# A gated linear recurrence with a two-branch maximum layer: the issue order of all queues remade, eleven float32 products on zeros at other places

## The chip, the cores and the metric

The kernel runs on one core of a Trainium2 chip. The core has five engines that run side by side, each with a queue of its own that is worked off in order: TensorE (PE in the profile, with PEld for its weight loads), VectorE (DVE), ScalarE (ACT), GpSimd (POOL) and SyncE (SP), which here only issues transfers. Sixteen DMA engines move data between HBM and the core. The metric is the device time of one execution in microseconds (us).

## The reference

The input has 4 batches, 8 heads, 768 time steps and 48 values per head. For every batch and head a 48 x 48 state is carried over the steps, and the result goes through a layer with two weight matrices, a maximum and an output matrix:

```
f = 1.0 / (1.0 + np.exp(-f_logit))
for t in range(S):
    state = f[:, :, t, :, None] * state + np.einsum('bhd,bhe->bhde', k[:, :, t], v[:, :, t])
    y[:, :, t] = np.einsum('bhd,bhde->bhe', q[:, :, t], state)
x = y.transpose(0, 2, 1, 3).reshape(B * S, H * D)      # 3072 x 384
g = np.maximum(x @ w1, x @ w2)                         # w1, w2: 384 x 1024
out = g @ w_out                                        # w_out: 1024 x 384
```

## The kernel before, in words

**Pieces.** The 768 steps of a batch are cut into three windows of 256, which makes 12 pieces, numbered 0 to 11; piece s belongs to batch s mod 4. A piece is one row of partitions for every two time steps, and its two halves of 128 steps (64 partitions each) are two links of the recurrence. The maximum is computed as `max(a, b) = b + relu(a - b)`: one product with w1 - w2 (called wd), a relu, and two products that end in one sum, with w_out and with w2 @ w_out (called m2). wd and m2 are made on the chip, once, at the start.

**Steps.** Every piece of work is a word of the string ORDER. Its letters name a step, then come the numbers of the piece (and of the part), a letter for the engine where there is a choice (a = ACT, v = DVE, p = POOL, s = SP), and `@` with a PSUM bank or an SBUF slot. A loop at the end of the kernel (`for key, of, e, b in words(ORDER)`) calls the steps in that order. There is no other scheduler: the order of the words of one engine is the order of its queue, and waits between engines follow from the data and from the reuse of banks, slots and buffers.

- Loads, all on SP: `Lf Lk Lq Lv` bring f_logit, k, q or v of one piece (393 KB, L137) into one of 22 slots; `Wa Wb` bring half of w1 or w2 (786 KB, L151), `Wo` half of w_out (L155). A load into a slot waits until the slot's earlier content has been read.
- Gates: `E F G` on ACT (exp, log, exp; L275, L279, L283), `e` adds two rows (L286), `C` is the product that sums the logarithms along time (L290, L293), `X Z` on ACT take the exponentials inv and dec (L300, L305).
- Scaled inputs: `i j` scale the even rows of k and q in place (L309, L313), `K Q` write bf16 copies scaled by inv and dec (L320, L323), `V` writes v as bf16 in three copies (L114).
- Recurrence: `t u` transpose K and Q on PE into two banks (L349), `U` copies both to SBUF (L114), `A` are the products of the two (L376), `m` masks them (L384), `S` multiplies with the state (L406), `y` with the values (L426); `D` makes what is added to the state (L440), `n N` update it (L452, L454, L457). `z` reads one column of each bank that `S` wrote, so that the reading engine is in step.
- Layer: `H Y` bring y into the layout of x (L114, L472), `d` with four parts is x times wd (L484), `r` the relu over two parts (L491, L493), `o` the two products that end in one sum (L499, L502), `b` copies it to SBUF (L114), `O` stores it (L520). The last half piece is stored in two halves of columns: `P B R` (L530, L533, L114, L541). `R` issues one transfer on SP and one on ACT's queue.
- Weights: `ws wp we` make wd (L575, L583, L114), `wc wt wx` transpose w2 (L114, L551), `wo` casts w_out, `wm wn` make m2 (L567, L114).
- `J` with a count: products of a 128 x 128 tile of zeros with four copies of itself in float32 (L595), into a bank that is then overwritten. They compute nothing that is used. A float32 product appears as two matmul instructions in the trace.

Of the kernel before, what the change touches and what calls it, by code (L numbers as in the profile page):

```python
# [17 lines left out]


ORDER = """  # L20
Lf0s@12 Lk0s@13 Lq0s@14 Lv0s@15 J4@7 E0a Wb0s F0a Lf1s@12 G0a i0v Wb1s e0v C0@0 J2@7 Wa0s X0a Wa1s
Z0a K0v V0p j0v t0@0 J1@7 Lq1s@13 D0@2 Q0v Lv1s@15 n0.0v u0@0 J2@7 E1a n0.1v U0v@0 F1a e1p A0.0@0
wc1a A0.1@2 m0.0v@0 S0@4 G1a Lk1s@12 wc0a C1@6 z0v@4 wt1@7 ws1v wc2a m0.1v@2 wp1@0 wx1a@7 ws3v y0
Z1a Wo0s ws0v we1a@0 wp3@2 H0a@4 ws2v wt2@7 we3a@2 Wo1s wp0@0 j1v X1a wp2@2 Y0v@4 Q1p we0a@0
Lf2s@0 wt0@6 wx2a@7 we2v@2 d0.0@0 d0.1@1 i1v V1a K1v d0.2@2 Lf4s@13 r0.0a@0 u1@4 wx0v@6 t1@4 wo1p
d0.3@3 U1v@4 wo0p D1@0 r0.1a@2 Lq2s@9 n1.0v A1.0@6 A1.1@4 wo3a wo2v S1@2 n1.1v Lk2s@10 m1.0v@6
wm0@0 E2a z1v@2 m1.1v@4 Lv2s@11 wm2@1 F2a E4a e2p y1 Lk4s@0 F4a C2@4 H1v@2 wm1@5 Y1v@2 Z2a e4p G2a
Lq4s@13 wn0a@0 C4@6 X2a d1.0@2 i2v wn2a@1 j2v wn1a@5 d1.1@3 Lf3s@8 Z4a Q2v d1.2@0 X4a G4a K2v
d1.3@1 V2a Lf5s@9 u2@4 t2@4 r1.1a@0 i4v o0.0@6 U2v@4 K4p Lv4s@11 r1.0a@2 j4v A2.0@0 b0.0a@6
Lq3s@10 D2@2 N1.1p o0.1@4 n2.0v E3a m2.0v@0 Q4p Lv3s@0 F3a n2.1v S2@0 b0.1a@4 A2.1@2 z2v@0 E5a  # L30
t4@6 N0.1p m2.1v@2 Lk3s@13 u4@6 N2.1p o1.0@5 F5a U4v@6 V4a Lf6s@9 e5v G5a y2 j3v b1.0a@5 D4@2
A4.0@6 H2a@0 O0s n4.0v o1.1@5 m4.0v@6 N4.0p Lk5s@11 V3a e3p Lv5s@8 n4.1v G3a Y2v@0 C5@6 b1.1a@5
C3@7 i3p X5a S4@2 Z3a A4.1@4 Lq5s@0 z4v@2 d2.0@0 Z5a Q3v X3a d2.1@1 E6a K3v d2.2@6 r2.0a@0 m4.1v@4
d2.3@7 Lq6s@13 t3@0 r2.1a@6 u3@0 i5p y4 D3@4 U3a@0 Lk6s@9 H4v@2 K5p o2.0@6 n3.0v Y4v@2 Lf8s@10 F6a
n3.1v S3@0 b2.0v@6 A3.0@2 e6p A3.1@4 m3.0v@2 d4.0@6 Lf7s@11 N4.1p d4.1@7 j5v V5p d4.2@2 z3v@0
r4.0a@6 Lk8s@12 m3.1v@4 d4.3@3 G6a D5@6 Q5v r4.1a@2 y3 O1s C6@5 j6v H3a@0 o2.1@4 Lv6s@0 Z6a i6v
E8a Y3v@0 Lq8s@8 X6a F8a t5@2 N3.1v u5@2 b2.1v@4 Lv7s@10 d3.0@0 U5a@2 e8v d3.1@1 n5.0v Q6v d3.2@4
K6v E7a d3.3@5 Lq7s@13 C8@2 N5.0v r3.1a@4 o4.0@3 r3.0v@0 V6p F7a Lf10s@9 n5.1v G8a e7v N5.1p D6@0
Z8a A5.0@4 b4.0v@3 X8a t6@6 Lf9s@0 j8v u6@6 C7@2 U6a@6 n6.0v o3.0@3 m5.0v@4 N6.0p Lk7s@11 V7p
n6.1v X7a i8v A5.1@0 b3.0a@3 A6.0@6 S5@4 Lf11s@10 j7v Z7a K8p o3.1@3 z5v@4 m5.1v@0 Lq9s@15 m6.0v@6  # L40
y5 S6@0 Q8v H5a@4 Lv8s@12 A6.1@6 G7a o4.1@2 E9a z6v@0 i7p m6.1v@6 F9a Y5v@4 b3.1a@3 y6 e9p E10a
O3s t8@6 u8@6 K7p H6a@0 d5.0@3 Lk9s@9 U8v@6 G9a Lq10s@0 b4.1a@2 C9@5 d5.1@4 X9a O4s Y6v@0 Z9a
N6.1p d5.2@6 r5.0a@3 O2s d5.3@7 Q7v d6.0@0 r5.1a@6 Lk11s@11 j9v A8.0@2 Lq11s@13 Q9p D7@4 V8a
m8.0v@2 u7@6 t7@6 d6.1@1 U7a@6 n7.0v Lv9s@12 d6.2@2 N7.0v n7.1v d6.3@3 j10v E11a o5.0@4 r6.0v@0
r6.1a@2 N7.1v A7.0@0 Lv11s@10 b5.0a@4 D8@2 A7.1@6 F11a n8.0v S7@4 m7.0v@0 o6.0@3 F10a e11p
Lk10s@15 G10a z7v@4 N8.0p m7.1v@6 e10p C11@0 Lv10s@8 b6.0a@3 S8@1 i9v A8.1@6 V9p o5.1@3 z8v@1
m8.1v@6 K9v C10@6 y7 Z10a b5.1v@3 D9@7 j11v H7a@4 y8 O5s Z11a Y7v@4 o6.1@3 X11a Q11p H8a@1 n9.0v
Y8v@1 d7.0@4 b6.1a@3 i10p G11a d7.1@5 O6s i11v d8.0@0 r7.0a@4 Q10v d8.1@1 N9.0v X10a d8.2@2 V10a
K10v d8.3@3 r8.0a@0 K11v d7.2@4 d7.3@5 r8.1v@2 u10@6 r7.1a@4 t9@0 u9@0 t10@6 t11@2 U9a@0 U10v@6
u11@2 o8.0@4 U11v@2 A9.0@0 b8.0a@4 S9@2 m9.0v@0 A9.1@6 D10@4 o7.1@5 z9v@2 m9.1v@6 V11v A11.0@0 y9  # L50
n10.0v D11@6 o7.0@4 n11.0v m11.0v@0 N11.0p H9v@2 o8.1@0 b7.0v@4 N10.0v b7.1a@5 Y9v@2 O7s A10.0@6
b8.1a@0 S10@4 m10.0v@6 A10.1@2 d9.0@0 z10v@4 d9.1@1 m10.1v@2 d9.2@6 r9.0a@0 d9.3@7 A11.1@0 r9.1a@6
S11@2 y10 z11v@2 m11.1v@0 o9.0@6 H10a@4 Y10v@4 y11 b9.0a@6 d10.0@0 H11v@2 d10.1@1 d10.2@4 r10.0v@0
o9.1@6 Y11v@2 d10.3@5 d11.0@0 r10.1a@4 d11.1@1 b9.1a@6 d11.2@2 O9s d11.3@3 O8s o10.0@4 r11.1v@2
r11.0v@0 o10.1@3 o11.0@0 b10.0a@4 b10.1a@3 O10s P11.0@1 b11.0a@0 O11s P11.1@0 B11.0v@1 R11.0s
B11.1a@0 R11.1s
"""


# [10 lines left out]
def kernel(  # L70
# [14 lines left out]
    nc = tc.nc  # L85
    B, H, S, D = q.shape
    C = 128
# [17 lines left out]
    banks = psum.tile([C, 8, 512], F32, name="banks")  # L105
# [18 lines left out]
    def load(nm, s, e, slot):  # L124
        w, b = divmod(s, B)
        rows = slice(w * W, (w + 1) * W)
        if s % 2 == 0 and (nm, s + 1) not in alone:

            n = 2
            src = sources[nm][b:b + 2, :, rows, :].rearrange("b h (p two) d -> (b h) p (two d)", two=2)  # L130
            dst = slots[:, slot:slot + 2, :].rearrange("p s (h x) -> p (s h) x", h=H)
            dst = bass.AP(dst.tensor, dst.offset, [list(dst.ap[i]) for i in (1, 0, 2)])
        else:
            n = 1
            src = sources[nm][b, :, rows, :].rearrange("h (p two) d -> p h (two d)", two=2)
            dst = slots[:, slot, :].rearrange("p (h x) -> p h x", h=H)
        engines[e].dma_start(out=dst, in_=src)  # L137
        for i in range(n):
            loaded[s + i][nm] = slots[:, slot + i, :].rearrange("p (h two d) -> p h two d", h=H, two=2)
# [20 lines left out]
    idle = consts.tile([C, C], F32, name="idle")  # L160
# [101 lines left out]
    m2 = consts.tile([C, KT, HD], BF16, name="m2")  # L262
# [327 lines left out]
        ps = banks[:, b:b + 2, :].rearrange("p b x -> p (b x)")[:, 0:KT * n]  # L590
        copy(e, wd[:, :, part * n:(part + 1) * n], ps.rearrange("p (k x) -> p k x", k=KT))

    def step_J(n, b):
        for _ in range(n):
            nc.tensor.matmul(out=banks[:, b, :], lhsT=idle, rhs=idle.unsqueeze(1).to_broadcast([C, 4, C]), start=True, stop=True)  # L595

    steps = {
        "J": lambda n, e, b: step_J(n, b),
        "Lf": lambda s, e, b: load("f", s, e, b), "Lk": lambda s, e, b: load("k", s, e, b),
        "Lq": lambda s, e, b: load("q", s, e, b), "Lv": lambda s, e, b: load("v", s, e, b),  # L600
        "Wa": lambda i, e, b: load_columns(w1_f, moe_w1, e, i),
# [59 lines left out]
```

## Time and profile before

| | |
|---|---|
| median of 3 runs | 140.78 us (140.59 to 141.03) |
| the profiled execution | 140.61 us, of which the span from the first to the last instruction is 138.8 us |
| PE busy in the span | 129.0 us (93%), 2349 matmuls |
| DVE, ACT, POOL busy | 110.1, 87.2, 47.2 us |
| HBM read, written | 23.59 MB, 4.72 MB |
| DMA engines | busy over nine tenths from slice 2 to slice 29 of 40 |

The profile is one execution. A line of a group names the kernel's line, engine, operation, what it writes and reads, the count, then the busy time, the mean of one in ns, and the idle time of the engine just before. Times in timelines count from the start of the span. "Issue" is time in which an engine waited for nothing that the profile shows. A matmul's end is modelled, so its start is the better mark.

### The profile page before, as it was taken

The page shows a single profiled execution, that of the slowest core. Times are in us where ns is not written, and L with a number is a line of the kernel's source. Part 1 is how long each engine was busy: PE and PEld are TensorE (multiplying, and loading weights), DVE is VectorE, ACT ScalarE, POOL GpSimd, SP SyncE. Part 2 cuts the span into 40 slices and gives each one's busy share as a digit, 9 for nine tenths or more (in the row PEclk, how much of TensorE's full clock was granted, in tenths as well). Part 3 has the DMA queues.
Part 4 walks back from the last instruction along what each step waited for, and adds up shares of the span by engine and source line. Part 5 has one row for each costly group of instructions (what it writes and reads, how often), then busy time and mean ns, then how long its engine had stood idle before and what let it go on. Part 6 is the DMA issues. An engine that isn't in the chain of part 4 may idle for free.

```text
span 138.8 us, 5409 instructions
## 1 busy us (share of the span) xinstructions
PE 129.0 (93%) x2349; PEld 92.1 (66%) x2349; DVE 110.1 (79%) x197; ACT 87.2 (63%) x145; POOL 47.2 (34%) x68
## 2 busy tenths in 40 slices
PE   6968779897999999999999999999999999999990
PEld 3335469564866687768666787677886668678570
DVE  5677799996978997999999899799888894861510
ACT  3623899659988989499883999716873115304220
POOL 7434205405096348610583943476200100000000
PEclk9999999999999999999999999999999999999999
DMA  4999999999999999999999999999500021000754
GB/s 104 272 326 341 387 288 285 357 257 250 266 264 253 275 275 252 246 288 260 237 271 217 245 235 313 279 269 228 126 0 5 5 56 58 5 5 20 209 130 97
DMA packets 56248, 28.66 MB, mean 206 GB/s; under 512 B 50464, under 2 KB 54688, under 8 KB 56224
## 3 DMA queue, kind: packets, MB, share of 16 engines
q1 hardware_dynamic: 56064, 28.22, 81.2%
q8 instruction: 18, 0.29, 0.9%
q10 hardware_dynamic: 160, 0.10, 0.3%
q14 instruction: 6, 0.05, 0.1%
HBM read 23.59 MB, written 4.72 MB: 204 GB/s over the span
## 4 chain that ended last, share of the span: by engine, by line
PE 74%; DMA 9%; ACT 4%; issue 4%; DVE 3%; POOL 2%; SPq 1%; ACTq 0%; DVEq 0%; POOLq 0%
PE banks L502 22%; PE banks L484 21%; PE banks L499 9%; DMA slots<-in_moe_w_dram 6%; PE banks L349 4%; PE banks L376 4%; PE banks L426 4%; PE banks L406 3%; DMA slots<-in_f_logit_dram 3%; PE banks L440 2%; PE banks L290 2%; ACT wd L114 1%; POOL wo L114 1%; SPq L151 1%; PE banks L567 1%
## 5 line engine op out<-in xcount | busy, mean ns | idle before, releaser
L502 PE MATMUL banks<-wo,gT 128*128 128x384 bf16 x184 | 33.7, 326 | 0.0
L484 PE MATMUL banks<-xT,wd 128*128 128x256 bf16 x288 | 33.6, 273 | 0.0
L384 DVE TENSOR_TENSOR at_m<-banks,mask 128x1024 bf16<-128x1024 f32 x24 | 29.0, 1216 | 1.5 <-PE banks L376 1.0
L484 PEld LDWEIGHTS <-wd 128*128 128x128 bf16 x288 | 27.3, 98 | 3.8
L502 PEld LDWEIGHTS <-gT 128*128 128x128 bf16 x184 | 18.0, 98 | 11.9
L491 ACT ACTIVATE gT<-banks 128x1024 bf16<-128x1024 f32 x18 | 18.4, 1032 | 11.9 <-PE banks L484 11.5
L114 ACT COPY ob<-banks 128x384 f32<-128x384 f32 (+1 forms) x19 | 8.9, 468 | 19.7 <-PE banks L502 14.5
L499 PE MATMUL banks<-m,xT 128*128 128x384 bf16 x69 | 15.1, 328 | 0.0
L472 DVE SCALAR_TENSOR_TENSOR xT<-tail,gaps,banks 128x256 bf16<-128x256 bf16 x36 | 15.0, 471 | 0.0
L275 ACT ACTIVATE gate<-slots 128x768 f32<-128x768 f32 x12 | 10.2, 847 | 7.0 <-DMA slots<-in_f_logit_dram 7.0
L114 POOL CAST vb<-slots 128x384 bf16<-128x384 f32 (+2 forms) x15 | 8.5, 604 | 12.1 <-DVE state L457 7.0
L457 POOL TENSOR_TENSOR state<-tmp_s,dec 128x256 bf16<-128x256 f32 x10 | 6.8, 680 | 17.2 <-DVE tmp_s L452 17.2
L286 POOL TENSOR_TENSOR e<-ell 128x384 bf16<-128x384 f32 x8 | 8.0, 999 | 13.2 <-ACT ell L279 13.2
L595 PE MATMUL banks<-idle 128*128 128x512 f32 x18 | 10.8, 738 | 1.1 <-DVE idle L161 1.1
L493 DVE TENSOR_SCALAR gT<-banks 128x1024 bf16<-128x1024 f32 x6 | 7.2, 1217 | 4.3 <-PE banks L484 4.3
L323 POOL TENSOR_TENSOR qp<-slots,dec 128x768 bf16<-128x768 f32 x4 | 7.3, 1818 | 9.6 <-DVE slots L313 6.7
L376 PE MATMUL banks<-trs 48*64 48x128 bf16 x384 | 10.1, 220 | 0.3 <-DVE trs L114 0.3
L279 ACT ACTIVATE ell<-gate 128x768 f32<-128x768 f32 x12 | 10.0, 846 | 0.4
L114 ACT COPY trs<-banks 128x2048 bf16<-128x2048 bf16 x5 | 9.3, 1864 | 0.3 <-PE banks L349 0.3
L114 DVE COPY trs<-banks 128x2048 bf16<-128x2048 bf16 x7 | 8.4, 1218 | 1.3 <-PE banks L349 1.3
L376 PEld LDWEIGHTS <-trs 48*64 48x64 bf16 x384 | 7.1, 106 | 3.5 <-issue 2.0
L320 POOL TENSOR_TENSOR kp<-slots,inv 128x768 bf16<-128x768 f32 x4 | 7.5, 1864 | 3.7 <-DVE slots L309 3.5
(76 smaller groups left out, 199.8 us busy)
## 6 DMA issues: line engine op xcount, KB each, us to landing
slots<-in_f_logit_dram SPq DMA_DIRECT2D x12, 384.0 KB, 5.9
slots<-in_k_dram SPq DMA_DIRECT2D x12, 384.0 KB, 5.8
slots<-in_q_dram SPq DMA_DIRECT2D x12, 384.0 KB, 5.9
slots<-in_v_dram SPq DMA_DIRECT2D x12, 384.0 KB, 5.8
out_dram<-ob SPq DMA_DIRECT2D x22, 192.0 KB, 3.1
slots<-in_moe_w_dram SPq DMA_DIRECT2D x4, 768.0 KB, 8.5
slots<-in_moe_w_out_dram SPq DMA_DIRECT2D x2, 768.0 KB, 7.5
out_dram<-ob SPq DMA_DIRECT2D x2, 96.0 KB, 2.2
```

The lines of the kernel that those rows point to most:

```text
L114: (nc.scalar.copy if e == "a" else engines[e].tensor_copy)(out, in_)
L275: nc.scalar.activation(flat(gate[s]), flat(loaded[s]["f"]), AF.Exp, bias=0.0, scale=-1.0)
L279: nc.scalar.activation(flat(ell[s]), flat(gate[s]), AF.Ln, bias=1.0, scale=1.0)
L286: engines[e].tensor_add(pad("e", s)[:, :, 0:D], ell[s][:, :, 0, :], ell[s][:, :, 1, :])
L376: nc.tensor.matmul(out=ps[h * HC:(h + 1) * HC, j % 2, par, :], lhsT=t[rows, 0, h, j, par, :], rhs=t[rows, 1, h, j], start=True, stop=True, ...
L384: nc.vector.tensor_mul(at[s][:, jj].rearrange("p r j a t -> p (r j) (a t)"), banks[:, b:b + 2, :].rearrange("p r (j x) -> p (r j) x", j=2) ...
L472: engines[e].scalar_tensor_tensor(out=x[:, kt], in0=tails[s], scalar=gaps[:, kt:kt + 1], in1=ps[:, :, kt], op0=ALU.mult, op1=ALU.add)
L484: nc.tensor.matmul(out=ps[:, f, :], lhsT=wd[:, kt, ff * C:(ff + 1) * C], rhs=xT[g][:, kt, :], start=(kt == 0), stop=(kt == KT - 1))
L491: nc.scalar.activation(dst, src, AF.Relu)
L499: nc.tensor.matmul(out=ps, lhsT=xT[g][:, kt, cols], rhs=m2[:, kt, :], start=(kt == 0), stop=False)
L502: nc.tensor.matmul(out=ps, lhsT=gT[g][:, ff, cols], rhs=wo[:, ff, :], start=False, stop=(ff == FG - 1))
L595: nc.tensor.matmul(out=banks[:, b, :], lhsT=idle, rhs=idle.unsqueeze(1).to_broadcast([C, 4, C]), start=True, stop=True)
```

## The change

The string ORDER is written anew: nearly every word stands elsewhere. The amount of each kind of step is the same; what differs is the order, many engines, banks and slots, and the zero products. `J` gets a width, and a second step `I` makes the same product with two copies of the tile in place of four, half as wide. Before there were nine zero products, all of `J` (4, 2, 1 and 2); after there are seven of `J` (4, 2 and 1) and four of `I` (1, 1 and 2), eleven in all.

The engines' shares change like this (steps, before and after):

| step | before | after |
|---|---|---|
| K on DVE, POOL | 8, 4 | 5, 7 |
| Q on DVE, POOL | 8, 4 | 6, 6 |
| i on DVE, POOL | 8, 4 | 3, 9 |
| V on ACT, DVE, POOL | 6, 1, 5 | 7, 5, 0 |
| b on ACT, DVE | 18, 5 | 13, 10 |
| r on ACT, DVE | 18, 6 | 21, 3 |
| H on ACT, DVE | 8, 4 | 6, 6 |
| N on DVE, POOL | 6, 10 | 5, 11 |
| wo on ACT, DVE, POOL | 1, 1, 2 | 3, 1, 0 |
| wc on ACT, DVE | 3, 0 | 2, 1 |
| wn on ACT, DVE | 3, 0 | 2, 1 |
| ws on DVE, POOL | 4, 0 | 3, 1 |

The diff, with the opening and the end of the order:

```diff
@@ -18,42 +18,42 @@
 ORDER = """
-Lf0s@12 Lk0s@13 Lq0s@14 Lv0s@15 J4@7 E0a Wb0s F0a Lf1s@12 G0a i0v Wb1s e0v C0@0 J2@7 Wa0s X0a Wa1s
-Z0a K0v V0p j0v t0@0 J1@7 Lq1s@13 D0@2 Q0v Lv1s@15 n0.0v u0@0 J2@7 E1a n0.1v U0v@0 F1a e1p A0.0@0
-wc1a A0.1@2 m0.0v@0 S0@4 G1a Lk1s@12 wc0a C1@6 z0v@4 wt1@7 ws1v wc2a m0.1v@2 wp1@0 wx1a@7 ws3v y0
-Z1a Wo0s ws0v we1a@0 wp3@2 H0a@4 ws2v wt2@7 we3a@2 Wo1s wp0@0 j1v X1a wp2@2 Y0v@4 Q1p we0a@0
-Lf2s@0 wt0@6 wx2a@7 we2v@2 d0.0@0 d0.1@1 i1v V1a K1v d0.2@2 Lf4s@13 r0.0a@0 u1@4 wx0v@6 t1@4 wo1p
-d0.3@3 U1v@4 wo0p D1@0 r0.1a@2 Lq2s@9 n1.0v A1.0@6 A1.1@4 wo3a wo2v S1@2 n1.1v Lk2s@10 m1.0v@6
-wm0@0 E2a z1v@2 m1.1v@4 Lv2s@11 wm2@1 F2a E4a e2p y1 Lk4s@0 F4a C2@4 H1v@2 wm1@5 Y1v@2 Z2a e4p G2a
-Lq4s@13 wn0a@0 C4@6 X2a d1.0@2 i2v wn2a@1 j2v wn1a@5 d1.1@3 Lf3s@8 Z4a Q2v d1.2@0 X4a G4a K2v
-d1.3@1 V2a Lf5s@9 u2@4 t2@4 r1.1a@0 i4v o0.0@6 U2v@4 K4p Lv4s@11 r1.0a@2 j4v A2.0@0 b0.0a@6
...
-b8.1a@0 S10@4 m10.0v@6 A10.1@2 d9.0@0 z10v@4 d9.1@1 m10.1v@2 d9.2@6 r9.0a@0 d9.3@7 A11.1@0 r9.1a@6
-S11@2 y10 z11v@2 m11.1v@0 o9.0@6 H10a@4 Y10v@4 y11 b9.0a@6 d10.0@0 H11v@2 d10.1@1 d10.2@4 r10.0v@0
-o9.1@6 Y11v@2 d10.3@5 d11.0@0 r10.1a@4 d11.1@1 b9.1a@6 d11.2@2 O9s d11.3@3 O8s o10.0@4 r11.1v@2
-r11.0v@0 o10.1@3 o11.0@0 b10.0a@4 b10.1a@3 O10s P11.0@1 b11.0a@0 O11s P11.1@0 B11.0v@1 R11.0s
-B11.1a@0 R11.1s
+J4@7 Lf0s@12 Lk0s@13 Lq0s@14 Lv0s@15 E0a Wb0s F0a Wa0s G0a e0v Lf1s@12 i0v C0@0 J2@7 Z0a j0v X0a
+Wb1s Q0v Wa1s K0v u0@0 I1@7 V0v t0@0 I1@7 Lk1s@13 U0v@0 D0@6 I2@3 n0.0v A0.0@0 A0.1@2 m0.0v@0 S0@4
+J1@0 ws0p z0v@4 Lq1s@15 m0.1v@2 E1a ws1v y0 wp0@0 Lv1s@12 H0a@4 n0.1v F1a Y0v@4 N0.1p wp1@2 we0a@0
+e1p we1v@2 wc1a C1@0 wc0v d0.0@6 wc2a ws2v wt1@1 Wo1s d0.1@7 G1a ws3v Z1a wt0@2 i1p r0.0a@6 wp2@3
+wx1v@1 Wo0s X1a wt2@5 we2a@3 j1v wp3@6 Lf2s@0 Q1v wx0a@2 d0.2@0 K1v u1@3 we3a@6 V1v wx2a@5 t1@3
+d0.3@1 U1v@3 Lf4s@13 D1@6 wo2a n1.0v A1.0@2 S1@4 m1.0v@2 wo3a r0.1a@0 Lk2s@10 z1v@4 A1.1@2 wo1a
+wo0v n1.1v Lq2s@11 m1.1v@2 wm0@0 E2a Lv2s@9 y1 F2a wn0v@0 wm1@3 H1v@4 E4a Y1v@4 Lq4s@0 G2a wm2@0
+F4a e2v i2v Lf3s@13 C2@4 e4v d1.0@1 X2a j2v wn1a@3 C4@5 K2v d1.1@2 Lk4s@8 Z2a wn2a@0 d1.2@6 Q2v
+r1.0a@1 d1.3@7 Lf5s@10 V2v Z4a u2@0 G4a t2@0 j4v r1.1a@6 D2@2 U2v@0 o0.0@4 Lv4s@9 Q4p E3a n2.0v
+Lq3s@11 o1.0@0 F3a i4v G3a e3p b0.0v@4 Lk3s@0 X4a n2.1v A2.0@6 b1.0a@0 S2@4 K4p A2.1@2 E5a z2v@4
+m2.0v@6 C3@0 Lf6s@13 o0.1@1 F5a m2.1v@2 V4a e5p Lv3s@8 t4@6 Z3a b0.1v@1 u4@6 X3a D4@2 j3v y2 U4a@6
+n4.0v Lq6s@9 C5@0 H2v@4 N4.0p o1.1@1 Y2v@4 N1.1p Lk5s@10 Z5a i3p X5a n4.1v S4@6 b1.1a@1 K3p A4.0@4
+E6a z4v@6 A4.1@2 Lq5s@12 m4.0v@4 d2.0@0 d2.1@1 V3a N4.1p m4.1v@2 Lf8s@0 d2.2@4 r2.0a@0 Q3p d2.3@5
+y4 Lf7s@8 r2.1a@4 D3@0 N2.1p t3@2 n3.0v H4a@6 u3@2 G5a o2.0@4 Y4v@6 Lv5s@11 U3a@2 i5p j5v Lk6s@13
...
+U10v@2 o7.0@5 U11v@0 b8.0v@7 A11.0@6 b7.0a@5 A10.0@0 m11.0v@6 d9.0@2 d9.1@3 N11.0v d9.2@5 m10.0v@0
+r9.0a@2 d9.3@6 S10@0 A10.1@2 z10v@0 o8.1@7 m10.1v@2 r9.1v@5 S11@2 y10 b8.1v@7 A11.1@5 z11v@2
+H10a@0 o9.0@7 Y10v@0 m11.1v@5 d10.0@0 d10.1@1 d10.2@5 r10.0a@0 d10.3@6 b7.1a@4 y11 O7s o9.1@4
+H11a@2 r10.1a@5 Y11v@2 O8s o10.0@5 d11.0@0 d11.1@1 d11.2@2 r11.0a@0 d11.3@3 b9.0a@7 o10.1@6
+r11.1a@2 b9.1v@4 O9s b10.0a@5 o11.0@7 b10.1v@6 O10s P11.0@6 b11.0a@7 O11s P11.1@7 B11.0v@6
+B11.1a@7 R11.0s R11.1s
 """
@@ -590,12 +590,14 @@
-    def step_J(n, b):
+    def step_J(n, b, w):
         for _ in range(n):
-            nc.tensor.matmul(out=banks[:, b, :], lhsT=idle, rhs=idle.unsqueeze(1).to_broadcast([C, 4, C]), start=True, stop=True)
+            nc.tensor.matmul(out=banks[:, b, 0:w * C], lhsT=idle, rhs=idle.unsqueeze(1).to_broadcast([C, w, C]),
+                             start=True, stop=True)

     steps = {
-        "J": lambda n, e, b: step_J(n, b),
+        "J": lambda n, e, b: step_J(n, b, 4),
+        "I": lambda n, e, b: step_J(n, b, 2),
```

## The prediction

> **What bounds the kernel now.** First the page's slices: PE is at nine tenths nearly throughout, and so are the DMA engines up to slice 29, so I asked when each of them sets the pace. The table of stretches, split where PE stops waiting and where its last products begin, answers (busy time of each engine with its count, granted clock, DMA share, GB/s):
>
> ```profile
> 0.00:35.10 35.10, 28.93 (x410) 17.94 (x411) 27.61 (x61) 23.17 (x38) 13.42 (x30) 1.00 1.06 287
> 35.10:97.00 61.90, 61.90 (x1338) 45.43 (x1337) 57.16 (x97) 49.68 (x86) 32.30 (x37) 1.00 1.08 259
> 97.00:134.30 37.30, 37.30 (x600) 28.05 (x599) 24.96 (x40) 14.01 (x22) 1.52 (x2) 1.00 0.22 52
> 134.30:138.80 4.50, 0.87 (x11) 0.64 (x8) 0.36 (x1) 0.32 (x1) 0.00 (x0) 0.95 0.53 133
> ```
>
> From 35.1 to 134.3 us PE is busy 99.2 of 99.2 us. All its waits lie in the opening, while the loads come in. So a new order can save something only before 35 us or after the last product; in between it can only add waits. The timeline of the opening's end shows what PE waited for there:
>
> ```profile
> 28.70 2.77 PE L567 MATMUL banks<-wo,w2T 128*128 128x384 bf16 x16
> 31.40 0.77 PE L426 MATMUL banks<-at_m,vb 64*64 64x128 bf16 x32
> 33.17 0.32 PE L290 MATMUL banks<-e,u_inc 128*128 128x384 bf16 x1 [1.00 <-POOL e L286]
> 33.33 0.24 PE L293 MATMUL banks<-ones,e 128*128 128x2 bf16 x4
> 33.43 1.46 PE L567 MATMUL banks<-wo,w2T 128*128 128x384 bf16 x8
> 34.84 0.32 PE L290 MATMUL banks<-e,u_inc 128*128 128x384 bf16 x1
> 35.00 0.24 PE L293 MATMUL banks<-ones,e 128*128 128x2 bf16 x4
> 35.10 2.78 PE L484 MATMUL banks<-xT,wd 128*128 128x256 bf16 x24
> 37.82 0.41 PE L349 MATMUL banks<-ident,qp 64*128 64x64 bf16 x16
> 38.06 0.40 PE L349 MATMUL banks<-ident,kp 64*128 64x64 bf16 x16
> 38.39 0.66 PE L499 MATMUL banks<-m,xT 128*128 128x384 bf16 x3
> ```
>
> Two `wm`, `y1`, a wait for `e2` on POOL, C2, the third `wm`, C4, d1, u2 and t2, then o0.0 at 38.39. Behind that wait stands the load of f2. The transfers' own view, one issue at a time (issue start plus time to landing), gives these landings: f0 4.6, k0 6.1, q0 7.7, v0 9.1, first half of w2 11.2, f1 12.6, other half 14.6, w1 16.7 and 18.8, then q1 21.3, v1 22.7, k1 24.1, w_out 26.2 and 28.4, f2 30.3, f4 31.7, then 33.0, 34.6, 36.0, 37.5, 39.0 and so on: one every 1.4 us (2.1 for a weight half), without a break.
>
> **What the Trainium skill says.** "TensorE: Matmul & The Clock Gate", What's actually happening: PE starts at half clock and reaches the full one after some 3.4 us of activity. The trace agrees, though the column of the granted clock reads 1.00: the first zero products' weight loads start 0.86 us apart up to 4.62 and 0.43 us apart from 5.34. Both orders begin with the same four J, so the clock is full at about 5 us in both, and the trace shows no later slow stretch even though PE is busy only 2.18 of 4 us from 16 to 20. "DMA: Bandwidth & Descriptors", Issuing engines are not separate DMA queues: all transfers share 16 engines; the DMA share above 1.0 up to 97 us fits. I therefore give the nth load the nth landing time, weights weighted, whatever its name. "SBUF — State Buffer", Who interferes with whom: a DVE operation with two SBUF inputs contends with POOL's reads. The trace agrees in a small way: L313 took 0.86 us beside POOL's casts at 9.9, 0.55 alone.
>
> **Part 1, the zero products.** A J costs 2 x 0.43 us. Before 9 x 0.86 = 7.7; after 7 x 0.86 + 4 x 0.43 = 7.7. Nothing, and all lie before 15 us, where PE waits for `U`, `m` or data. If that cover went, each costs its own 0.43 or 0.86.
>
> **Part 2, load order.** Same bytes, same issuing queue. w1's first half moves ahead of f1, k1 ahead of q1, the halves of w_out swap. Landings: w1 13.3, f1 14.7, w2 16.7, w1 18.8, k1 21.3, q1 22.7, v1 24.1, w_out 26.2 and 28.4, f2 30.3, f4 31.7, k2 33.0, q2 34.6, v2 36.0, q4 37.5, f3 39.0, k4 40.5, f5 42.0, v4 43.9. The load of f2 waits for `ws2` (19.9 us below; before it was issued at 22.0), so it isn't later.
>
> **Part 3, the opening, walked queue by queue.** Durations are the trace's: on DVE m 1.22, U 1.22, Y 1.27, K and Q 0.96, ws 0.95, i and j 0.56, n 0.42, V 0.85; on ACT E, F 0.85, r 1.03, wx 1.13, wo 0.83, X, Z, G 0.5. Independent neighbours start some 0.08 us before the end of the one ahead (m at 29.29 and 30.49), a dependent start costs 0.04.
>
> - Piece 0: `e0` ahead of `i0` gives C0 at 7.0 (8.03 before). On DVE from q0's landing: j0 7.7, Q0 8.3, K0 9.2, V0 10.1, U0 10.7 to 11.9, n0.0 to 12.25, m0.0 12.7 to 13.95 (15.11 before), m0.1 to 15.2. y0 ends at 15.5.
> - Piece 0 into the layer: H0 15.7, Y0 16.3 to 17.6, C1 18.2, d0.0 18.4 (22.95 before). This lead of 4.5 us is worth little: next come piece 1 and w_out, which wait for their loads.
> - Piece 1 on DVE: j1 22.75 (q1), Q1, K1, V1 to 25.8, U1 25.75 to 26.95, n1.0, m1.0 to 28.7, wo0 to 29.25, n1.1, m1.1 to 30.7. On ACT: wo2 26.25 (its load), wo3, r0.1 to 28.8, wo1 to 29.55.
> - So wm0 starts near 29.5 (28.70 before). From there PE has work without a wait: wm0 1.3, y1 0.6, wm1 1.3, wm2 1.3, that is to 34.1. C2 needs e2, now on DVE: H1 32.1, Y1 to 33.35, e2 to 33.8. C2 ends at 34.35, d1.0 at 35.05, C4 (e4 34.8) at 35.3, d1.1 to d1.3 at 37.35.
> - K2 from 35.2, Q2 to 37.0, V2 to 37.65. u2 37.35, t2 to 37.95, D2 to 38.5, and o0.0 starts at 38.5.
>
> Before, o0.0 started at 38.39 with D2 still to do (0.5 us). **Gain: 0.4 us** of PE work. The margins are thin: Q2 is 0.35 us early, V2 0.3, C4's e4 0.25.
>
> **Part 4, the dense stretch.** I walked on to `o4.1`: each PE step had its inputs, but by 0.1 to 1 us only (V4 for D4, U4 for S4, m3.0 for A3.1, POOL's Q3 for u3). The engines' shares favour the new order: from the table in the change, with the groups' means, DVE loses 3 K, 2 Q, 5 i, 3 r (2.9 + 1.9 + 3.0 + 3.7) and gains 4 V, 5 b, 2 H (3.4 + 2.8 + 0.8), about -5 with the rest; POOL gains 3 K, 2 Q, 5 i (5.6 + 3.6 + 5.0) and loses 5 V and 2 wo (9.0 + 1.7), with the rest +6 of 47; ACT +1.4. No engine gets near PE's 99 us. But PE can't beat 100% busy, and some 200 hand-overs lie in new places. I take 0.3 us of small waits (nothing to 2.5).
>
> **Part 5, the end.** Before, R11.0's transfer stood on ACT's queue ahead of B11.1; now both R stand behind it:
>
> ```profile
> 134.36 0.36 DVE L114 COPY ob<-banks 128x192 f32<-128x192 f32 x1 [3.97 <-PE banks L533]
> 134.75 0.55 ACTq L541 DMA_DIRECT2D out_dram<-ob  x1
> 135.18 1.19 SPq L541 DMA_DIRECT2D out_dram<-ob  x2
> 135.34 0.32 ACT L114 COPY ob<-banks 128x192 f32<-128x192 f32 x1 [1.42 <-PE banks L533]
> 135.69 0.48 ACTq L541 DMA_DIRECT2D out_dram<-ob  x1
> ```
>
> B11.1 could start at 135.27 (0.1 after the last product, as the DVE copy does), then ACT issues R11.0 (135.6 to 136.15) and only then R11.1 (136.2). SP's two issues don't move: they stand behind O11. The last transfer starts at 136.2 in place of 135.8 on SP: **+0.35 us** (0.1 to 0.5).
>
> **Sum.** 138.8 - 0.4 + 0.35 + 0.3 = 139.05 us of span; 1.8 us lie around it (140.61 - 138.8) and the median was 0.17 above that run: 141.0 us. That is no change: 0.3% (0.42 us) is about what this measurement can tell.
>
> **Rivals.**
>
> - *A, 34%: as walked*, 141.0, own range 140.4 to 141.2.
> - *B, 26%, slower: a feeder comes late in the dense stretch.* POOL's chain for piece 3 is the likeliest place: N4.0 (after n4.0, 46.5), N1.1, i3, K3, N4.1, Q3 one after the other, 0.7 + 0.7 + 1.0 + 1.9 + 0.7 + 1.8 = 6.8, ends at 53.3; u3 is due at 53.95. It decides once the chain is over 0.7 us late. One load's step (1.4 us, k3) with 0.6 of contention makes it 2.0 late: 1.3 us of wait, 142.3. For it: seven K at 1.86 us on POOL, and ACT's 1.86 us U3 behind. Against: o2.0 (1.85 us) covers U3.
> - *C, 22%, faster: the walk is too careful.* The first products of wm0 need only wo0, 29.25: 0.3 us earlier. With no wait later and a tail of 0.1: 138.8 - 0.7 + 0.1, so 140.2. It decides if V2 ends before 37.4. Against: the loads hold q2 and v2 back to 34.6 and 36.0.
> - *D, 13%, slower: DVE is late in the opening.* If its starts don't overlap, 30 operations x 0.08 put e2 at 35 in place of 33.8; C2, C4, u2 and D2 then wait, 1.2 us together: 142.2. It decides if Y1 ends after 34. Before, POOL did `V0`, two `wo` and `e2`; these are now DVE's or ACT's.
> - *E, 5%: the clock falls to half* in the sparse stretch from 16 to 28. 3.4 us at half speed lose 1.7: 142.7. Against: the trace of before at 16 to 20.
>
> The change can't fail to act: the queues differ from their first words.
>
> **Numbers.** A gives the forecast and "same". C is faster: 22%. B, D and E are slower: 44%. Range: below, C with both gains and no small wait, 139.9; above, B and D at their priced ends with part of each other, 142.9.
>
> **What would show it.** C0 at 7.0, m0.0 at 12.7, wm0 near 29.5, C2 near 34.1 and o0.0 near 38.5 with D2 done confirm part 3. A PE total below its span between 38.5 and 134 shows B, at the line that it names; products of L484 over 0.2 us apart show E. If loads land later than the list (a slot still read), everything after 22 us is wrong. If the last transfer on ACT's queue starts within 0.4 us of B11.1's end, part 5 is wrong.

## The result and the profile after

The changed kernel took 142.79 us (median of 4; 142.14 to 144.4) where the kernel before took 140.85 us (median of 4; 140.59 to 141.03). The ratio is 1.0123, with a 95% interval of 1.0074 to 1.0173: slower by 1.2%, some 1.9 us. Measured again beside the experiments it was 1.0168 (1.0118 to 1.0218). Ratios leave out the executions that are over 1.5% above the fastest of their kernel; medians of times have all of them. The profiled execution was the longest of the four, 144.4 us with a span of 142.6 us; the spans of the other three were 140.4 to 141.3 us, and what is read below from its dense stretch is more than theirs.

First the table of stretches of the changed kernel, cut as before and then finely from 28 us on (busy time and count of PE, PEld, DVE, ACT, POOL, then granted clock, DMA share, GB/s):

```profile
0.00:35.10 35.10, 29.43 (x395) 17.79 (x396) 28.34 (x67) 21.38 (x33) 8.79 (x25) 0.95 1.03 280
35.10:97.00 61.90, 60.83 (x1285) 43.98 (x1284) 51.32 (x91) 50.63 (x89) 39.30 (x34) 1.00 1.07 252
...
134.30:142.60 8.30, 4.57 (x39) 3.31 (x37) 0.92 (x2) 1.46 (x4) 0.00 (x0) 1.00 0.58 142
28.00:30.50 2.50, 0.57 (x17) 0.37 (x17) 1.51 (x4) 2.50 (x4) 0.00 (x0) 1.00 0.95 208
...
31.00:31.50 0.50, 0.50 (x3) 0.24 (x2) 0.50 (x1) 0.44 (x1) 0.00 (x0) 0.57 1.17 304
31.50:34.00 2.50, 2.50 (x38) 1.32 (x37) 1.05 (x3) 2.47 (x5) 0.00 (x0) 0.50 0.91 228
...
34.50:35.00 0.50, 0.50 (x4) 0.29 (x3) 0.50 (x2) 0.15 (x1) 0.00 (x0) 1.00 1.09 290
```

The column to read is the clock. It was 1.00 throughout the opening of the kernel before; here the opening's mean is 0.95, and the fine rows show where that comes from. From 28 to 30.5 us PE was busy for 0.57 of 2.5 us. From about 31.07 us (the row of 31.0 has 0.57, so some 0.43 us of it at half) to about 34.5 us the clock was 0.50: 3.4 us. PE was fully busy through these 3.4 us.

The timeline of PE in the changed kernel shows what fell into them (start, length, operation; in brackets the idle time before and who ended it):

```profile
28.73 0.42 PE L376 MATMUL banks<-trs 48*64 48x128 bf16 x16 [0.98 <-DVE at_m L384]
30.34 2.37 PE L567 MATMUL banks<-wo,w2T 128*128 128x384 bf16 x8 [1.20 <-DVE wo L114]
32.64 1.07 PE L426 MATMUL banks<-at_m,vb 64*64 64x128 bf16 x32
33.64 3.17 PE L567 MATMUL banks<-wo,w2T 128*128 128x384 bf16 x16
36.65 0.33 PE L290 MATMUL banks<-e,u_inc 128*128 128x384 bf16 x1
...
40.46 0.45 PE L440 MATMUL banks<-vb,kp 64*64 64x64 bf16 x32
40.84 0.34 PE L499 MATMUL banks<-m,xT 128*128 128x384 bf16 x1
```

Two idle stretches, 0.98 and 1.20 us, stand around the 16 short products of `A1.1`. Then `wm0` takes 2.37 us where the kernel before took 1.46 us for the same 8 products (its `wm1`), and `y1` 1.07 in place of 0.77 us. Everything after is late by as much: o0.0 starts at 40.84 us in place of 38.39, with `D2` (0.38 us) already done here and not there. So the opening lost 2.07 us (2.45 - 0.38).

The second wait, 1.20 us for `wo`, is seen in the timelines of ACT (three lines) and of DVE in the changed kernel:

```profile
27.57 1.56 ACT L114 CAST wo<-slots 128x768 bf16<-128x768 f32 x2 [1.46 <-DMA slots<-in_moe_w_out_dram]
29.04 1.02 ACT L491 ACTIVATE gT<-banks 128x1024 bf16<-128x1024 f32 x1
29.96 0.82 ACT L114 CAST wo<-slots 128x768 bf16<-128x768 f32 x1
```

```profile
29.73 0.56 DVE L114 CAST wo<-slots 128x768 bf16<-128x768 f32 x1 [0.99 <-DMA slots<-in_moe_w_out_dram]
```

ACT casts the half of w_out that landed first, `wo2` and `wo3`, at 27.57; but `wm0` begins with `wo0`, and DVE can cast that only when the other half has landed, at 29.7.

Of the 3.8 us by which this span is longer, 2.07 lie before o0.0, 1.07 in the dense stretch as waits (60.83 busy of 61.90 us, where there was none before), 0.1 after the last product, and the remaining 0.56 is PE's work in the dense stretch, spread over it.

### The profile page after: what moved, and what is told of

Its sections match the earlier page's. It is cut to its first block, busy times and chain, and to the rows that moved or that the text cites. A ratio compares the mean times of both kernels' runs of the same rounds, so it can differ in the third digit from the quotient of the medians.

```text
span 142.6 us, 5412 instructions
## 1 busy us (share of the span) xinstructions
PE 132.1 (93%) x2353; PEld 92.7 (65%) x2353; DVE 107.0 (75%) x203; ACT 87.4 (61%) x144; POOL 53.5 (37%) x63
## 4 chain that ended last, share of the span: by engine, by line
PE 85%; DMA 6%; ACT 2%; DVE 1%; issue 1%; SPq 1%
PE banks L502 21%; PE banks L484 21%; PE banks L499 9%; PE banks L595 8%; DMA slots<-in_moe_w_out_dram 6%; PE banks L426 5%; PE banks L349 5%; PE banks L376 4%; PE banks L567 4%; PE banks L406 3%; PE banks L440 3%; PE banks L290 2%; SPq L155 1%; PE banks L533 1%; DVE at_m L384 1%
## 5 line engine op out<-in xcount | busy, mean ns | idle before, releaser
L484 PE MATMUL banks<-xT,wd 128*128 128x256 bf16 x288 | 34.4, 273 | 0.0
L484 PEld LDWEIGHTS <-wd 128*128 128x128 bf16 x288 | 27.1, 98 | 3.8
L491 ACT ACTIVATE gT<-banks 128x1024 bf16<-128x1024 f32 x21 | 21.6, 1028 | 11.5 <-PE banks L484 11.3
L323 POOL TENSOR_TENSOR qp<-slots,dec 128x768 bf16<-128x768 f32 x6 | 11.3, 1885 | 18.9 <-PE banks L349 18.3
L472 DVE SCALAR_TENSOR_TENSOR xT<-tail,gaps,banks 128x256 bf16<-128x256 bf16 x36 | 15.1, 475 | 3.8 <-ACT tail L114 3.7
L499 PE MATMUL banks<-m,xT 128*128 128x384 bf16 x69 | 15.1, 328 | 0.0
L320 POOL TENSOR_TENSOR kp<-slots,inv 128x768 bf16<-128x768 f32 x7 | 12.7, 1817 | 4.4 <-ACT inv L300 4.3
L595 PE MATMUL banks<-idle 128*128 128x512 f32 (+1 forms) x22 | 12.3, 692 | 1.9 <-DVE idle L161 1.1
L114 ACT COPY ob<-banks 128x384 f32<-128x384 f32 (+1 forms) x14 | 6.5, 468 | 11.8 <-PE banks L502 10.4
L114 DVE COPY ob<-banks 128x384 f32<-128x384 f32 (+1 forms) x11 | 5.9, 534 | 8.0 <-PE banks L502 5.9
L309 POOL TENSOR_TENSOR slots<-slots,one 128x384 f32<-128x384 f32 x9 | 9.2, 1018 | 3.6 <-DMA slots<-in_k_dram 2.4
L305 ACT ACTIVATE dec<-banks 128x392 f32<-128x392 f32 x12 | 5.9, 500 | 6.4 <-PE banks L293 6.4
```

Source lines behind the costliest of these rows:

```text
L114: (nc.scalar.copy if e == "a" else engines[e].tensor_copy)(out, in_)
L320: engines[e].tensor_mul(pad("kp", s)[:, :, :, 0:D], by_parity(loaded[s]["k"]), both(inv[s]))
L323: engines[e].tensor_mul(pad("qp", s)[:, :, :, 0:D], by_parity(loaded[s]["q"]), both(dec[s][:, 0:HD].rearrange("p (h d) -> p h d", h=H)))
L472: engines[e].scalar_tensor_tensor(out=x[:, kt], in0=tails[s], scalar=gaps[:, kt:kt + 1], in1=ps[:, :, kt], op0=ALU.mult, op1=ALU.add)
L484: nc.tensor.matmul(out=ps[:, f, :], lhsT=wd[:, kt, ff * C:(ff + 1) * C], rhs=xT[g][:, kt, :], start=(kt == 0), stop=(kt == KT - 1))
L491: nc.scalar.activation(dst, src, AF.Relu)
```

## The experiments

The main theory (Theory 1): the order leaves PE nearly idle for some 2.5 us just ahead of the point from which it sets the pace, the clock falls, and the first 3.4 us of dense work run at half of it. The rivals: loads wait for their slots, so that w_out comes late (Theory 2, no clock in it); w_out comes late because of the order of the loads (Theory L); or the new order is dearer in the dense stretch. Each ratio below is against the kernel before on the same chip. There its executions spread over 140.6 to 144.05 us, with medians of 141.4 to 141.8 us. Two chips were used: the changed kernel once more, four more zero products, the other slots and the kernel before without five zero products ran on one, all others on the second. The changed kernel itself was not timed on the second, so a comparison of those others with its 1.0168 goes from chip to chip. Of each edit only the words that change are shown, with a neighbour or two.

**The changed kernel once more** (no edit).

> The changed kernel once more, beside the kernel before on the same chip. Theory 1 (the clock): in the sparse stretch from 27.7 to 30.3 us PE does too little, the granted clock falls to half for one stretch of 3.4 us and PE loses 1.7 us. Then the slices 28 to 36 us show a clock near 0.5 again, and the time is 142 to 143 us. Theory 2 (the loads): the halves of w_out land 1.3 us later than before (27.6 and 29.7), and that alone makes it slow; then the clock may be full in this profile and the time is still 142 to 143 us. If the half clock comes in some executions only, times lie far apart (over 1 us).

It took 143.66 us, ratio 1.0168. All 6 executions had a mean clock of 0.973 to 0.988, as all 4 of the first measurement had (0.982 to 0.988). In its profile the clock was at half from about 29.8 to 36.6 us, 6.8 us: twice as long as in the first profile. So the fall is no accident of one execution, but its length varies.

**Four more half-wide zero products in the gap.**

```diff
-A1.0@2 S1@4 m1.0v@2
+A1.0@2 S1@4 I2@6 m1.0v@2
-A1.1@2 wo1a
+A1.1@2 I2@6 wo1a
```

> The changed kernel with four more half-wide zero products (0.43 us each) in the stretch in which PE idles: two after S1, two after A1.1, into a bank that is free there. Theory 1: the clock stays full, 1.7 us less, 140.8 us. Theory 2: no difference, 142.5 us, or up to 0.4 us more where a zero product is in the way.

Ratio 1.0055 (1.0031 to 1.0080), 142.29 us; all 22 executions had a clock of 0.994 or more. The timeline of PE in this kernel:

```profile
27.87 1.13 PE L595 MATMUL banks<-idle 128*128 128x256 f32 x4
...
29.28 1.13 PE L595 MATMUL banks<-idle 128*128 128x256 f32 x4
30.89 1.63 PE L567 MATMUL banks<-wo,w2T 128*128 128x384 bf16 x8 [0.48 <-DVE wo L114]
32.45 0.64 PE L426 MATMUL banks<-at_m,vb 64*64 64x128 bf16 x32
```

The zero products fill what was idle, `wm0` is back at 1.63 us and `y1` at 0.64, and o0.0 starts at 39.82 us with `D2` done: 1.02 us sooner, although `wm0` itself began 0.55 us later (w_out landed that much later in this execution: the cast of `wo0` started at 30.27 us in place of 29.73). Work that computes nothing made the kernel faster by some 1.1% (1.0168 to 1.0055).

**Only the first of these two pairs** (`I2@6` after `S1@4`).

> The changed kernel with only the first pair of zero products added, after S1 (0.86 us of work); after A1.1 PE still idles for over 1 us. Clock theory: the busy share of the stretch from 27.6 to 31 us decides, so this lies between the changed kernel and the one with both pairs: 0.5 to 1.3% over the kernel before, with a full clock in some executions and a half one in others. If one pair is enough: 0.5%. If only a gap's length counts, and the longest gap is what is left after A1.1 (1.2 us): 1.2 to 1.7%.

Ratio 1.0007 (0.9981 to 1.0032), 142.05 us; clock 0.994 or more in all 24 executions, `wm0` at 30.55 and o0.0 at 39.37. This is better than expected. Two half-wide products are enough to keep the clock; the second pair adds nothing that shows. Six of the 24 executions took 143.6 to 144.5 us although their clock was full. The profiled one is among them; its PE waits 2.2 us in the dense stretch for nothing that the profile shows.

**The same eleven zero products, three of them elsewhere.** The `I2` after `D0` (two half-wide products) and the `J1` after `S0`, all in the first 17 us, move to the gap; nothing is added.

```diff
-D0@6 I2@3 n0.0v
+D0@6 n0.0v
-J1@0 ws0p
+ws0p
-A1.0@2 S1@4 m1.0v@2
+A1.0@2 S1@4 I2@6 m1.0v@2
-A1.1@2 wo1a
+A1.1@2 J1@6 wo1a
```

> The changed kernel with the same eleven zero products, three of them moved: the two half-wide ones behind D0 go behind S1 (27.7 us), the full one behind S0 goes behind A1.1 (29.2 us). Clock theory: only where they stand counts. The clock is full from 28 us on and the time is that of the kernel with four products added, 0.3 to 0.9% over the kernel before (141.2 to 142.0 us). If instead the clock falls where the products were taken away, the slices from 14 to 20 us show it, and as PE waits for data there it costs under 0.5 us. If it takes more zero products, not other places, the clock falls at 31 us as in the changed kernel and the time is 1.2 to 1.7% over.

Ratio 1.0025 (1.0000 to 1.0051), 142.2 us. With the same amount of such work, most of the loss is gone: the place decides. 8 of 22 executions still had a clock of 0.982 to 0.988, but here it cost next to nothing: their median is 142.36 us, that of the others 142.2 us. No profile shows where it fell in them. In the profiled execution, which kept its clock, PE is now least busy from 11.7 to 15.1 us (1.47 us of 3.4), where the zero products were taken away, and not ahead of `wm0`.

**Other slots for three loads.** k1, q1 and v1 go into slots that nothing else uses, so that no load up to w_out waits for a read.

```diff
-Lk1s@13
+Lk1s@16
-Lq1s@15
+Lq1s@17
-Lv1s@12
+Lv1s@18
```

> The changed kernel with k, q and v of piece 1 loaded into three slots that nobody uses (16, 17, 18), so that these loads, and those of w_out behind them, wait for no reader. Theory 2: w_out lands at about 26.2 and 28.4 us, wm0 starts some 1.3 us earlier, and 0.7 to 1.3 us go: about 141.5 us. Theory 1: the gap before wm0 gets shorter, but if the clock still falls the time stays at 141.5 to 142.5; if the gap is short enough the clock holds and the time is 140 to 141 us, which the profile's clock tells apart.

Ratio 1.0078 (1.0049 to 1.0107), 142.99 us, but w_out landed at 27.8 and 30.0 us, not sooner than in the changed kernel (27.6 and 29.7). The theory of the slots falls. The run gave something better: its 22 executions are of two kinds. Eight had a clock of 0.994 or more, median 141.94 us; fourteen had 0.972 to 0.988, median 143.61 us. That is some 1.7 us for the fall of the clock, in one and the same kernel. The second kind takes as long as the changed kernel (143.66 us), and the first is still some 0.6 us above the kernel before (141.38 us). The ratio of 1.0078 understates the loss, since it leaves out six executions of the second kind. Its profile is of the first kind: `wm0` at 30.64, o0.0 at 39.52 with `D2` done, no wait of PE between there and the last product. And yet PE was as idle ahead of `wm0` as in the changed kernel:

```profile
28.00:30.50 2.50, 0.42 (x16) 0.25 (x15) 1.39 (x3) 2.50 (x4) 0.00 (x0) 1.00 1.17 257
```

So the sparse stretch alone doesn't settle it; what does is worked out in the last section.

**The kernel before without five of its nine zero products** (`J2`, `J1` and `J2` between 8 and 15 us).

```diff
-C0@0 J2@7 Wa0s
+C0@0 Wa0s
-t0@0 J1@7 Lq1s
+t0@0 Lq1s
-u0@0 J2@7 E1a
+u0@0 E1a
```

> The kernel before without its five zero products between 8 and 15 us (the first four stay), so PE idles there. Theory 1: a sparse stretch of PE takes the clock down to half for 3.4 us or more wherever it comes, so this falls too, somewhere from 9 to 20 us; as PE is mostly waiting there, it costs less than 1.7 us: 141 to 142 us. Rival to it: the clock in the changed kernel fell for a reason of its own (its dense products from 30 us on), and without these zero products the kernel before stays at full clock and at 140.8 us.

Ratio 1.0014 (0.9985 to 1.0042), 141.78 us, with a clock of 0.960 to 0.976 in all 12 executions. Its table of stretches:

```profile
8.00:12.00 4.00, 0.81 (x21) 0.64 (x21) 2.69 (x3) 0.88 (x2) 2.75 (x3) 0.80 1.12 330
12.00:20.00 8.00, 6.29 (x132) 4.84 (x135) 6.45 (x9) 6.95 (x11) 1.00 (x1) 0.50 1.10 354
```

Ten microseconds at half clock (10.41 to 20.65 us) cost nothing that can be measured (the interval leaves room for 0.6 us). PE waits for data there anyway: it was busy for 6.29 us of 8, and in the kernel before, with its zero products, for 6.17. So the fall of the clock is cheap early and dear where PE sets the pace, and what the zero products between 8 and 15 us gain in the kernel before is too little to be measured.

**The halves of w_out in the other order.** Half 0 is loaded first, ACT casts `wo0`, `wo1` and `wo3`, DVE casts `wo2`; `wm0` and `wn0` go to another bank, and the slots 8 to 11 are renamed to fit (that part is left out here).

```diff
-Wo1s
+Wo0s
-Wo0s
+Wo1s
-wo2a
+wo0a
-wo3a
+wo1a
-wo1a
+wo3a
-wo0v
+wo2v
-wm0@0
+wm0@6
-wn0v@0
+wn0v@6
```

> The changed kernel with the halves of w_out loaded and cast in the other order (the half that m2's sum uses first comes first), the slots 8 to 11 renamed to fit, and the first m2 product in bank 6. The zero products are untouched. Theory: PE's idle stretch before wm0 is what takes the clock down. Here the first four products of wm0 can start at about 29.4 us in place of 30.4, so the idle stretch is shorter and 0.65 us less work is left behind the late half: 0.6 us less, and if the clock holds thereby, 1.7 us less again, 140.3 us. If the clock has nothing to do with that stretch it still falls at 31 us and the time is 142.5 us.

Ratio 0.9994 (0.9964 to 1.0024), 141.98 us. The timeline of PE in this kernel:

```profile
29.02 0.42 PE L376 MATMUL banks<-trs 48*64 48x128 bf16 x16 [0.99 <-DVE at_m L384]
29.36 1.62 PE L567 MATMUL banks<-wo,w2T 128*128 128x384 bf16 x8
...
38.73 0.66 PE L499 MATMUL banks<-m,xT 128*128 128x384 bf16 x3
```

The first products of `wm0` now follow `A1.1` without a wait, since the half that they need first has landed first (27.2 us) and the other half (29.5) is cast before they come to it. PE is busy for 1.51 us from 28 to 30.5 in place of 0.57; the clock was at 0.988 in only 3 of 22 executions, and 1.00 in the profile. This single exchange takes the whole loss away. It does two things at once: `wm0` starts about 1 us sooner, and the clock is kept.

**f1 and both halves of w2 ahead of w1, as before the change.**

```diff
-F0a Wa0s G0a e0v Lf1s@12 i0v
+F0a Lf1s@12 G0a e0v Wb1s i0v
-Wb1s Q0v Wa1s K0v
+Wa0s Q0v Wa1s K0v
```

> The changed kernel with the load of f1 and the halves of w2 ahead of w1, as in the kernel before. Theory L (the new place of f1 holds up the issue of v1, and with it w_out): w_out lands near 26.2 and 28.4 us as before, and the time falls by about 1 us. Theory M (the new order of the loads has no part in it): w_out lands at 27.6 to 30 us again, and the time stays at 142.5 us or rises by up to 1 us, since wd's first parts come 1.4 to 3.4 us later and PE idles more in the opening.

This missed by far: ratio 1.0332 (1.0260 to 1.0404), 146.68 us. w_out did land sooner (26.6 and 28.6), as the theory of the load order said, but w1 landed at 17.8 and 19.9 in place of 13.1 and 19.6, and in this order of steps everything from wd on stands behind it. The table of stretches of this kernel:

```profile
20.00:26.00 6.00, 5.44 (x33) 4.05 (x33) 2.60 (x4) 3.50 (x5) 2.59 (x4) 0.50 1.04 280
...
28.00:32.00 4.00, 3.54 (x63) 2.83 (x60) 3.90 (x10) 4.00 (x11) 0.00 (x0) 1.00 0.33 86
```

After a stretch with 0.20 us of PE's work in 4 (16 to 20 us) came 6.8 us at half clock (19.74 to 26.56 us), now in a place where PE had a backlog; the slots of the weights were read later, the load of f2 was issued at 26.2 us in place of 21.8 and that of f4 at 31.0 in place of 25.2, and the DMA engines moved 86 GB/s from 28 to 32 us. `wm0` began at 35.10.

**The exchange of w_out, one pair of zero products and the end as before, together** (the edits of the exchange; `I2@6` after `S1@4`; and this):

```diff
-B11.1a@7 R11.0s R11.1s
+R11.0s B11.1a@7 R11.1s
```

> The kernel with w_out's halves in the other order, with two half-wide zero products after S1 (PE idles there for 1 us) and with the last piece's first transfers issued ahead of B11.1 as in the kernel before. Clock theory: full clock in the profile, and 0.1 to 0.4 us less than that kernel where that one has the full clock too: 140 us. If the clock falls nevertheless: 142 us.

Ratio 0.9997 (0.9971 to 1.0023), 141.66 us, clock 0.995 or more in all 22 executions. Nothing is gained over the exchange alone; the end's order isn't worth what can be measured.

**Two words of the kernel before, to find a faster one.** Its PE waited 1.00 us for `e2` on POOL; `e2` goes to DVE, and `d1.0` moves ahead of `C4`.

```diff
-e2p y1
+e2v y1
-C4@6 X2a d1.0@2 i2v
+d1.0@2 C4@6 X2a i2v
```

> The kernel before with two steps from the changed one: e2 on DVE in place of POOL, and d1.0 ahead of C4. PE waited for e2 from 32.2 to 33.2 us. Theory (only PE's waits in the opening can be won back): C2 starts near 32.7, d1.0 and C4 are done at 35.3 in place of 35.9, and 0.4 to 0.6 us go: 140.3 us. Rival: what PE wins there it waits later for loads, 140.8 us.

Ratio 0.9955 (0.9930 to 0.9981), 141.23 us: faster than both kernels, by a little under half a per cent against the kernel before. The timeline of PE in this kernel:

```profile
32.76 0.32 PE L290 MATMUL banks<-e,u_inc 128*128 128x384 bf16 x1
...
38.01 0.66 PE L499 MATMUL banks<-m,xT 128*128 128x384 bf16 x3
```

C2 starts at 32.76 without a wait (33.17 before, after 1.00 us), o0.0 at 38.01 (38.39).

## Why the prediction was right or wrong

The forecast was no change at 141.0 us; measured is a loss of 1.2%, 142.79 us. Its likeliest case didn't come. The case that came is rival E, which had a chance of 5%, a price of 1.7 us (about that was measured with other slots) and a time of 142.7 us. That 142.79 us lies just inside the stated range (up to 142.9) is luck: this end was priced from B and D, and neither came. That it lies so near to E's 142.7 us is in part luck too, since w_out came late as well, which E had not in it.

- **The step that failed** is in part 3: "From there PE has work without a wait: wm0 1.3, y1 0.6, wm1 1.3, wm2 1.3". By the walk's own times PE has little to do between `U1` (done at 26.95) and `wm0` (29.5): only `A1` and `S1`, and a wait for `m1.0` (28.7). But it priced what follows at full clock. `wm0` took 2.37 us, `y1` 1.07, `wm1` and `wm2` 3.17 together (2.77 with the clock kept).
- **The argument against E** was that 2.18 us of work in 4 didn't bring the clock down in the kernel before. That was true of 16 to 20 us in one execution and said nothing on 0.57 in 2.5 us; in the experiments 24 of 152 executions of the kernel before had a mean clock of 0.982 to 0.988. E was also looked for from 16 to 28 us, where it would have been nearly free at least up to 20.6 us, as the kernel before without five zero products shows. Its sign was misplaced likewise: `L484` products ran at full clock, `L567` didn't.
- **The Trainium skill** ("TensorE: Matmul & The Clock Gate", HAM oscillation — how this bites in real kernels) says that idle gaps of PE of over some 3.4 us, between bursts of products, bring it back to half clock. The prediction named from that page only how the clock rises. The trace agrees with the fall, but not with the condition: the longest idle gaps ahead of it were 0.98 and 1.20 us, with 0.42 us of work between. The prediction's "the clock is full at about 5 us in both" didn't hold either: in the changed kernel's profile the weight loads of the first zero products are still 0.85 us apart at 6.33 us, and these products take 6.73 us in place of 5.74.
- **Part 1** (zero products, nothing) counted their durations and their cover, and missed their other effect: what they do for the clock of the work behind them. Moving three of them was worth some 1.4% (1.0168 to 1.0025).
- **Part 2** (the nth load lands at the nth time) held to 0.2 us for the loads up to v1, except w1's second half (19.6 for 18.8), and failed for w_out: 27.6 and 29.7 in place of 26.2 and 28.4. With f1 and w2 ahead of w1 it is 26.6 and 28.6, in one profiled execution; in those with the new order of the earlier loads the first half landed at 27.2 to 28.1. So it depends on the order of the loads, and the slots of k1, q1 and v1 have no part in it. By which mechanism it depends on the order stays open.
- **Part 3, otherwise.** Piece 0 was 0.6 to 0.9 us late (C0 at 7.62 for 7.0, m0.0 at 13.62 for 12.7, d0.0 at 19.27 for 18.4), since the clock rose later and the four first zero products ended later with it; that was covered. `wm0` came at 30.34 for 29.5. Without a fall of the clock o0.0 is at 39.37 to 39.52 (one pair of zero products; other slots). With `D2` at 0.38 us (the walk took 0.5) that is 0.6 to 0.75 us of PE's work lost by the late w_out, where 0.4 was to be gained. With the halves exchanged it is at 38.73, next to no gain (38.39 + 0.38 - 38.73 = 0.04): there the walk's 38.5 was nearly right, and so was its "no change".
- **Part 4.** Rival B didn't come: POOL's K3 and Q3 ended at 55.4 us and u3 began on time at 56.38. The waits of PE from 35 to 134 us in the changed kernel are put down to nothing that the profile shows:

```profile
PE banks L349 <- issue: 0.7, 1, 0.7
PE banks L376 <- issue: 0.3, 1, 0.3
```

  Other kernels with the same order have 0 (other slots), 0.4 (halves exchanged), 0.5 (four zero products) and 2.2 us (one pair) of it in their profiled executions. These waits, 1.0 us together, are more than the 0.3 us that the walk took and within the "nothing to 2.5" that it allowed. But the cause that was named, inputs late by a hand-over, isn't seen in this profile. What it is stays open.
- **Part 5.** The two issues on ACT's queue stood as described, but cost 0.1 us in place of 0.35 (3.73 us from the last product's end to the end of the span, 3.63 before):

```profile
138.05 0.82 PE L533 MATMUL banks<-wo,gT 128*128 128x192 bf16 x8
...
138.91 0.32 ACT L114 COPY ob<-banks 128x192 f32<-128x192 f32 x1 [1.34 <-PE banks L533]
138.91 1.38 ACTq L541 DMA_DIRECT2D out_dram<-ob  x2
```

  The first transfer was issued beside `B11.1`'s copy, not behind it: both start at 138.91. The walk had put them in sequence.

In the prediction's own terms the sum becomes, for the profiled execution: +2.07 (some 1.65 from the clock: from `wm0`'s start to o0.0 it is 10.50 us here, and 8.82 and 8.88 where the clock was kept, with one pair and with other slots; the other 0.4 from the late w_out) for -0.4, +0.1 for +0.35, and +1.63 in the dense stretch for +0.3, together 3.8. What of the 1.63 the shorter executions have can't be told from their spans.

## What to carry to other kernels

After walking a new order queue by queue, look at what comes ahead of the place from which TensorE sets the pace, and add up how busy it is there in 3.4 us, wherever these begin. Where such a stretch can have less than some 2 us of work, price 3.4 us at half clock behind it, as a chance: here 24 of 32 executions paid it and 8 didn't. Fill the gap with useful products whose inputs can be brought there first (here by loading the other half of a weight first), and only then with zero products, as few as keep the clock. Where TensorE waits for data anyway, a low clock costs next to nothing, and zero products there are worth next to nothing.

## What the runs showed that I had not expected

- 0.57 us of work in 2.5 us, with no gap over 1.2 us, brought the clock to half in the changed kernel's profile; 0.42 in 2.5 with other slots didn't. So neither the gaps nor the sum alone decide.
- The Trainium skill (the same page, What's actually happening) says that activity is watched in a window of some 3.4 us that runs freely and doesn't start with the kernel. The traces agree. This table has the four profiles in which the clock fell. The falls and the rises behind them are read from the column of the clock in fine slices. When the clock first became full is an estimate: in the kernel before it is about 5.2 us, where the weight loads of the first zero products change from 0.86 to 0.43 us apart, and elsewhere twice as much later as these products take longer than there.

| profile | clock first full at | at half clock | for | from first full to the fall | PE busy in the 3.41 us ahead of the fall |
|---|---|---|---|---|---|
| the changed kernel | 7.2 us | 31.07 to 34.48 us | 3.41 us | 23.9 us (7 x 3.41) | 1.23 us |
| the changed kernel once more | 5.9 us | 29.81 to 36.64 us | 6.83 us (2 x 3.41) | 23.9 us (7 x 3.41) | 1.76 us |
| f1 and w2 ahead of w1 | 6.1 us | 19.74 to 26.56 us | 6.82 us (2 x 3.41) | 13.6 us (4 x 3.41) | 0.00 us |
| before, without five zero products | 7.0 us | 10.41 to 20.65 us | 10.24 us (3 x 3.41) | 3.4 us (1 x 3.41) | 1.48 us |

- So in each of these executions the clock changed only on a grid of 3.41 us, and the grid lies elsewhere from one execution to the next: the twelve profiles have the clock first full at 4.1 to 7.2 us, though their first product starts at 1.05 us in all. If the twelve are cut along their grids up to 42 us (in the eight without a fall the grid is counted from that estimate), every other piece at full clock has at least 2.05 us of PE's work. The limit here is thus between 1.76 and 2.05 us of 3.41. With other slots a line of the grid (at about 29.1 us) cuts the sparse stretch in two, with 2.17 and 2.09 us in the pieces, and the clock held. At half clock it stayed there after pieces with 1.20 to 2.59 us of work and rose after pieces with 3.35 us or more; hence 3.4 us in one execution and 6.8 us in another of the same kernel.
- An estimate from these profiles: if every position of the grid is as likely as any other, and less than 1.9 us in a piece brings the fall, the clock falls in about 7 of 10 executions of the changed kernel and of the one with other slots (24 of 32 had a mean clock under 0.99), in 2 of 10 of the kernel before (24 of 152), and in none with one pair of zero products, with two pairs or with the halves exchanged (3 of 68).
- Two half-wide float32 zero products (1.13 us in the timeline) prevented it in 24 of 24 executions.
- The order of three earlier loads moved the landing of w_out by 1.0 us with the same bytes ahead of it (one profiled execution of each).
